# Block-sparse attention and a maxout layer: the first third of three batches' attention rows transposed by TensorE in place of DMA transposes

## The chip, the cores and the metric

The kernel runs on one core of one Trainium2 chip. The metric is device time in microseconds (us) of one execution; of the kernel before there are three timed runs and one profiled execution. Engines are named as in the profile: PE (TensorE, with PEld for its weight loads), DVE (VectorE), ACT (ScalarE), POOL (GpSimd) and SP (SyncE, which here only issues transfers). ACT has a transfer queue as well.

## The reference

Four batches of eight heads attend over 768 positions with head size 64. Each position sees its neighbours closer than 16 and 24 block summaries (the maximum of 32 keys, the mean of 32 values). The result, laid out as 3072 rows of 512, goes through a maxout layer:

```python
k_sum = k.reshape(B, H, nb, 32, D).max(axis=3);  v_sum = v.reshape(B, H, nb, 32, D).mean(axis=3)
scores_l = where(|i - j| < 16, scale * q @ k.T, -1e9)
scores_s = scale * q @ k_sum.T + log(32)
a = softmax(concat([scores_l, scores_s]))
x = (a @ concat([v, v_sum])) laid out as (3072, 512)
out = maximum(x @ w1, x @ w2) @ w_out          # d_model 512, d_ff 1024
```

The kernel uses max(h1, h2) = h1 + relu(h2 - h1): it computes `x @ (w2 - w1)`, takes relu of it (tile `g`), and adds `x @ (w1 @ w_out)` to `g @ w_out`. The product `w1 @ w_out` is made once (tile `w1o`).

## The kernel before, in words

**The work.** For each batch b (0 to 3) and each pair of heads hp (0 to 3), `prep` loads q and k, casts them to bf16 (`cast`), turns them so that the head dimension lies on partitions (`turn`, L463: by PE into a PSUM bank; `dturn`, L467: by a DMA transpose, for six of the sixteen pairs, listed in `CFG["turn"]`), and places keys and block maxima (`place`, `max`, `sums`, `tails`, `wrap`). A batch's 768 positions are cut into three groups (grp 0 to 2) of 256, and each group is done in two halves of four heads. For each half: `scores` (L529), `exp` on ACT (L541), a mask multiplication on DVE (L549, batches 1 to 3), `values` (L569), a reciprocal of the row sums (L587) and their product, the tile x (L590, four blocks of 128 by 128, bf16).

**The step that is changed.** The layer needs x transposed (tile `xt`, one for each batch and group). In batch 0 PE does it: `turn x` is four transposes into a bank (L605), and DVE or ACT copies the bank into `xt` (L258, label `xt`). In batches 1 to 3 SP issues one DMA transpose for each half (L596, label `dxt`, 18 in all).

**The layer.** For each group: `hidden` (L678, four banks of eight products of 256 columns), relu on ACT or DVE (L690, L692), then for each 128 rows `out`: four products `x` with `w1o` and eight with `g` (L715; 512 columns each), a copy out of the bank (L258, `copy out`) and a `store` (L729, L731; on SP's or ACT's queue). The last 128 rows, "320" (batch 3, group 2, half 0), are made in three pieces of 256, 128 and 128 columns. `w1o` is made at L662 from `w1t` and `wo`.

**What sets the order.** Every step is a task in a plan. A table of numbers (`CFG["order"]`) gives the order in which the tasks are issued, a string (`CFG["engines"]`) gives each task's engine, and another (`CFG["slots"]`) which buffer of its ring it writes. Each engine takes its tasks in that order, and waits for what they read and for the buffers that they overwrite. There are 30 `filler` products (L750), which write zeros and are read by nobody; all but two stand on PE ahead of the first 22 us' end.

Of the kernel before, what the change touches and what calls it, by code (L numbers as in the profile page):

```python
# [18 lines left out]


CFG = dict(
    turn="22 23 30 31 32 33", fill=30, apart="",
)
CFG["engines"] = "".join("""
DDPDDDDPPDPDPDPPTTTTTTTTTTTTTTTTTTTTTTTTTTTTTTSSSPAAATDDPSSSADDATADDSSSDDDATAADSSSPPDPTDPDSSDATDSSPATDSSDDTASSDDTDSDSA
SPSDDTATADPPPDPTDTADPADDATDTDDPPPADTATDDPAADTTATTDDTATTATTDDTATTATTDDTDTTATTDDTDTTATTDDTDTTATTDDTASSSASSSDSSSDSSSPADDD
DPTAPDDDAADDDTDTDDPAAAATDTADDPPADTDTDDPAPDDTDTDDAADDTADTTDDSTADTTDDSTADTTDDSTADTTDDSTADTTDDSTADTTDDSSSSASSSASSSASSSADP
DAPAPTADADAPAPDATATDDPDADDTATDDPDPDPSDSDDPDPDSASADDPDTADTTDDSTADTTDDSTADTTDDSTADTTDDSTADTTDDSTADTTDDSSSSDSSSDSSSDSSSDP
ADPAAATAPPDDDPPAPSASDDDPPASASDDAPPPSDSDDADPDSDSADDPDTADTTDDSTADTTDDSTADTTDDSTADTTDDSTADTTDDSTADTTDDSTTATTDTTATTDTTATTA
TTDTTATTTAATTTASTTDTTDTTATTATTTDSTTTDSTTATTDTTATTDTTTAATTTAATATDTATATTTASTTTASTDTATATDTTTASTTTASTATATDTATTTAATTTASTDTA  # L30
TDTATTTAATTTDSTDTATATATTTDSTTTAATATDTATATTTASTTTAATDTATDTATTTASTTTAATDTDTDTDTTTDSTTTDATATATDTATTTAATTTAATTTDSTTTDS
""".split())
CFG["order"] = list(map(int, """
# [28 lines left out]
""".split()))  # L62
CFG["slots"] = "".join("""
62042222021106710531003202313307231146225:92038;61<0042111340176159:02011300112351100237323242320261022522460324040071
0001000221160432210551<47898;6372010411534153241633000262220121202324610426125432206020144162353<002=47:;8>50241030214
34123211222003301214111422034002204241064003223621;<21536:=01>97125053101142010320204231000000501212040203202124342346
2201623730702125441574016062035031561075120162776743420432132341762015540341624532677725412445001541265304420201127162
""".split())
ENG = {"T": "PE", "D": "DVE", "A": "ACT", "P": "POOL", "S": "SP"}

# [25 lines left out]
class Plan:  # L96
# [6 lines left out]
    def op(self, on, fn, read=(), write=(), change=(), touch=(), label=""):  # L103
        t = Task()
        n = t.index = len(self.tasks)
        t.alts, t.letter, t.fn, t.label = on, on[0], fn, label
        if self.engines:
            t.letter = self.engines[n]
            assert t.letter in on, (label, t.letter, on)
        t.new = [*dict.fromkeys((*write, *change))]  # L110
        t.deps = {w for b in (*read, *change) for w in b.writers}
        t.uses = [*dict.fromkeys((*read, *touch, *t.new))]
        for b in t.new:
            b.writers.append(t)
        for b in t.uses:
            b.users.append(t)
            if b.ring and not b.fixed and b not in self.bufs:
                self.bufs.append(b)
        self.tasks.append(t)
        return t  # L120
# [15 lines left out]
def kernel(  # L136
# [31 lines left out]
    def tiles(name, n, shape, dt):  # L168
        return [const.tile(shape, dt, name=f"{name}{i}") for i in range(n)]
# [24 lines left out]
    apart = tiles("apart", 2, [128, H, VW], BF16) if lone else ()  # L194
# [36 lines left out]
    def queue(e):  # L231
        return {"S": nc.sync, "A": nc.scalar, "P": nc.gpsimd}[e]
# [323 lines left out]
    def values(b, hp, grp, pb):  # L556
# [25 lines left out]
        inv, x, half = Buf(invr), Buf(xsr), hp // 2  # L582
        if hp == 0:
# [8 lines left out]
            in0=spread(bank_tile[:, ps.ap, 0:1], [512, 2], [D + 1, 4], [1, D]),  # L592
            in1=spread(inv.ap[:, 0:1, 0:1], [4, 2], [1, 4], [0, D]), op=ALU.mult),
           read=[ps, inv], write=[x], label=f"x {tag}")
        if b > 0:
            op("S", lambda e: queue(e).dma_start_transpose(  # L596
                out=x_t.ap[:, hp:hp + 2, :].rearrange("p h (u n) -> p (h u) n", u=2),
                in_=x.ap[:].rearrange("p h u a d -> p (h u a d)")),
               read=[x], write=[x_t, x_h], label=f"dxt {tag}")
            return  # L600
# [134 lines left out]
    def attention(b):  # L735
        for hp in range(NP):
            prep(b, hp)
        for grp in range(NG):
            for half in range(2):
                on_pe = b == 0  # L740
                ps = Buf(banks, "sc")
                scores(b, 2 * half, grp, ps, on_pe)
                pb = weigh(b, 2 * half, grp, ps, on_pe)
                values(b, 2 * half, grp, pb)
# [67 lines left out]
```

## Time and profile before

| | |
|---|---|
| timed runs | 164.91 us median of 3 (164.22 to 164.93) |
| profiled execution, its own time | 165.06 us |
| its span, first to last instruction | 163.2 us |
| PE busy, share of the span | 152.8 us, 94% |
| DVE, ACT, POOL busy | 111.5, 97.5, 43.9 us |
| granted PE clock | 1.0 |

The profile is read as follows: a row of a group gives the source line, the engine, the operation, what is written and read, the shapes and the count, then the busy time and the mean of one, then idle time of the engine ahead of it. L258 and L256 are the lines of a helper that makes every copy, so those rows are told apart by their tiles. A matmul's shown duration is longer than the step from one matmul to the next, since they are pipelined.

### The profile page before, as it was taken

The page shows a single profiled execution, that of the slowest core. Times are in us where ns is not written, and L with a number is a line of the kernel's source. Part 1 is how long each engine was busy: PE and PEld are TensorE (multiplying, and loading weights), DVE is VectorE, ACT ScalarE, POOL GpSimd, SP SyncE. Part 2 cuts the span into 40 slices and gives each one's busy share as a digit, 9 for nine tenths or more (in the row PEclk, how much of TensorE's full clock was granted, in tenths as well). Part 3 has the DMA queues.
Part 4 walks back from the last instruction along what each step waited for, and adds up shares of the span by engine and source line. Part 5 has one row for each costly group of instructions (what it writes and reads, how often), then busy time and mean ns, then how long its engine had stood idle before and what let it go on. Part 6 is the DMA issues. An engine that isn't in the chain of part 4 may idle for free.

```text
span 163.2 us, 4346 instructions
## 1 busy us (share of the span) xinstructions
PE 152.8 (94%) x1761; PEld 99.9 (61%) x1782; DVE 111.5 (68%) x220; ACT 97.5 (60%) x140; POOL 43.9 (27%) x95
## 2 busy tenths in 40 slices
PE   6977889999999999999999999999999999999990
PEld 2534668888645655588665745868554576686640
DVE  3469999997897899869988576454937967115000
ACT  3369898446529899993999435866659510043121
POOL 6725457003036020069250240000595000000000
PEclk9999999999999999999999999999999999999999
DMA  4999999998999999579899997699996523531752
GB/s 152 324 312 316 263 389 391 395 395 259 281 301 265 308 339 260 89 177 279 114 231 290 320 180 169 120 135 277 229 133 209 128 37 68 161 118 55 233 179 64
DMA packets 67988, 36.48 MB, mean 224 GB/s; under 512 B 54912, under 2 KB 61952, under 8 KB 67968
## 3 DMA queue, kind: packets, MB, share of 16 engines
q1 hardware_dynamic: 66048, 33.43, 77.0%
q10 hardware_dynamic: 1920, 2.77, 5.2%
q8 instruction: 14, 0.23, 0.6%
q14 instruction: 6, 0.05, 0.1%
HBM read 25.18 MB, written 6.29 MB: 193 GB/s over the span
## 4 chain that ended last, share of the span: by engine, by line
PE 55%; issue 15%; DMA 8%; SPq 7%; DVE 6%; POOL 5%; ACT 2%; POOLq 0%; DVEq 0%
PE banks L715 22%; PE banks L678 17%; PE banks L662 4%; SPq L336 4%; DMA land<-in_q_dram 3%; PE banks L569 3%; DMA land<-in_k_dram 3%; POOL vx L256 3%; PE banks L463 3%; PE banks L529 2%; DVE vx L258 2%; POOL kx L258 2%; DVE ks L487 2%; SPq L729 1%; DMA out_dram<-o 1%
## 5 line engine op out<-in xcount | busy, mean ns | idle before, releaser
L678 PE MATMUL banks<-xt,wd 128*128 128x256 bf16 x384 | 45.6, 273 | 0.0
L715 PE MATMUL banks<-wo,g 128*128 128x512 bf16 (+2 forms) x198 | 44.6, 362 | 0.9 <-issue 0.6
L678 PEld LDWEIGHTS <-wd 128*128 128x128 bf16 x384 | 36.9, 98 | 6.9 <-issue 0.3
L715 PEld LDWEIGHTS <-g 128*128 128x128 bf16 x208 | 19.2, 98 | 18.4
L690 ACT ACTIVATE g<-banks 128x512 bf16<-128x512 f32 x28 | 15.7, 596 | 22.2 <-PE banks L678 22.1
L541 ACT ACTIVATE pb<-banks 128x1024 bf16<-128x1024 f32 x24 | 23.7, 1029 | 8.4 <-PE banks L529 8.2
L715 PE MATMUL banks<-w1o,xt 128*128 128x512 bf16 (+2 forms) x96 | 23.6, 362 | 0.6 <-DVE kqb L258 0.2
L692 DVE TENSOR_SCALAR g<-banks 128x512 bf16<-128x512 f32 x20 | 13.5, 685 | 10.4 <-PE banks L678 10.3
L487 DVE TENSOR_REDUCE ks<-kx 128x24 bf16<-128x768 bf16 x16 | 14.9, 947 | 2.7 <-ACT kx L258 2.4
L590 DVE TENSOR_TENSOR xs<-banks,inv 128x512 bf16<-128x512 f32 x24 | 16.4, 689 | 0.5
L258 ACT COPY o<-banks 128x512 f32<-128x512 f32 (+1 forms) x18 | 10.0, 574 | 11.1 <-PE banks L715 7.6
L258 POOL COPY kx<-kx 128x32 bf16<-128x32 bf16 (+1 forms) x16 | 6.5, 422 | 35.9 <-ACT kx L258 20.7
L549 DVE TENSOR_TENSOR pb<-pb,mask 128x1024 bf16<-128x1024 bf16 x18 | 12.2, 693 | 4.3 <-ACT pb L541 4.0
L715 PEld LDWEIGHTS <-xt 128*128 128x128 bf16 x104 | 9.5, 98 | 8.8
L256 POOL COPY vx<-sums 32x396 bf16<-32x396 bf16 x18 | 9.6, 557 | 10.8 <-ACT vx L258 5.5
L750 PE MATMUL banks<-zeros,identity 128*128 128x512 bf16 x29 | 10.3, 465 | 1.6 <-DVE identity L239 1.6
L258 ACT CAST kqb<-land 128x768 bf16<-128x768 f32 x11 | 10.1, 937 | 2.6 <-DMA land<-in_k_dram 2.5
L463 PE MATMUL banks<-ident,kqb 128*128 128x128 f32 x60 | 10.2, 286 | 1.5 <-DVE sums L269 1.1
L258 ACT COPY vx<-vx 32x128 bf16<-32x128 bf16 (+5 forms) x12 | 10.2, 860 | 1.9 <-DVE vx L258 1.7
L463 PEld LDWEIGHTS banks<-ident,kqb 128*128 128x128 f32 x60 | 7.4, 145 | 5.1 <-DVE sums L269 1.5
L258 DVE CAST kqb<-land 128x768 bf16<-128x768 f32 x15 | 8.8, 607 | 2.5 <-DMA land<-in_q_dram 1.3
L258 DVE COPY o<-banks 128x512 f32<-128x512 f32 (+1 forms) x8 | 4.7, 591 | 8.0 <-PE banks L715 6.8
(82 smaller groups left out, 175.7 us busy)
## 6 DMA issues: line engine op xcount, KB each, us to landing
land<-in_k_dram SPq DMA_DIRECT2D x16, 384.0 KB, 5.7
land<-in_v_dram SPq DMA_DIRECT2D x14, 384.0 KB, 5.8
land<-in_q_dram SPq DMA_DIRECT2D x14, 384.0 KB, 5.5
land<-in_moe_w_dram SPq DMA_DIRECT2D x8, 512.0 KB, 8.8
out_dram<-o SPq DMA_DIRECT2D x12, 256.0 KB, 2.6
land<-in_moe_w_out_dram SPq DMA_DIRECT2D x4, 512.0 KB, 11.0
out_dram<-o ACTq DMA_DIRECT2D x7, 256.0 KB, 2.3
w1t<-in_v_dram SPq DMA_DIRECT2D x2, 384.0 KB, 5.3
```

The source lines that it names most:

```text
L256: nc.gpsimd.tensor_copy(out=o[:, n * z:n * z + n], in_=i[:, n * z:n * z + n])
L258: {"D": nc.vector.tensor_copy, "A": nc.scalar.copy, "P": nc.gpsimd.tensor_copy}[e](out=o, in_=i)
L463: nc.tensor.transpose(out=bank(ps)[:, 128 * j:128 * j + 128], in_=src.ap[:].bitcast(F32)[:, 128 * j:128 * j + 128], identity=ident32[:])
L487: op("D", lambda e: nc.vector.tensor_reduce(out=ks.ap[:, 0:nb], in_=free(kt(), 128, [256, NM], [192, 2], [32, 2], [1, 32]), axis=AX.X, op= ...
L541: op("A", lambda e: nc.scalar.activation(out=spread(pb.ap[:, 0, 0:1], [1, 1024]), in_=spread(bank_tile[:, ps.ap, 0:1], [1, 1024]), func=AC ...
L549: on(e).tensor_tensor(out=o.rearrange("p n (u c) -> p n u c", u=2), in0=o.rearrange("p n (u c) -> p n u c", u=2), in1=in1, op=ALU.mult)
L590: op("D", lambda e: nc.vector.tensor_tensor(out=x.ap[:].rearrange("p n u a d -> p n (u a) d"), in0=spread(bank_tile[:, ps.ap, 0:1], [512, ...
L678: nc.tensor.matmul(out=bank(ps)[:, 256 * s:256 * s + 256], lhsT=wd[n // 2][:, c, 256 * (n % 2) + 128 * s:256 * (n % 2) + 128 * s + 128], r ...
L690: nc.scalar.activation(out=o, in_=bank(ps), func=ACT.Relu)
L692: nc.vector.tensor_scalar_max(out=o, in0=bank(ps), scalar1=0.0)
L715: nc.tensor.matmul(out=bank(ps, c1 - c0), lhsT=a, rhs=w, start=(i == j == 0), stop=(i == 2 and j == 3))
L750: nc.tensor.matmul(out=bank(ps), lhsT=identity[:], rhs=zeros[:], start=True, stop=True)
```

## The change

For the groups listed in a new entry, `x="10 20 30"` (group 0 of batches 1, 2 and 3), the early return with the DMA transpose is not taken, so the two halves of each go through `turn x` and the copy `xt`, as in batch 0: six pieces. The task list grows from 822 to 828, and order, engines and slots are new tables. The source lines below the table move by two (L605 is L607 in the changed kernel, L715 is L717).

```diff
 CFG = dict(
-    turn="22 23 30 31 32 33", fill=30, apart="",
+    turn="22 23 30 31 32 33", fill=30, apart="", x="10 20 30",
 )
...
-46 57 8 18 3 48 27 79 10 36 9 58 31 0 1 6 11 13 12 24 2 14 26 68 28 122 15 35 4 59 40 123 132 37 47 126 21 42 127 128
...
+38 97 71 182 163 96 199 73 75 144 164 102 183 67 155 103 72 76 30 200 216 78 184 29 82 161 109 145 185 165 186 151 166
...
-        if b > 0:
+        if b > 0 and f"{b}{grp}" not in CFG["x"].split():
             op("S", lambda e: queue(e).dma_start_transpose(
                 out=x_t.ap[:, hp:hp + 2, :].rearrange("p h (u n) -> p (h u) n", u=2),
                 in_=x.ap[:].rearrange("p h u a d -> p (h u a d)")),
                read=[x], write=[x_t, x_h], label=f"dxt {tag}")
             return
```

The number of tasks on each engine goes from 291 to 297 on PE, 218 to 214 on DVE, 150 to 158 on ACT, 58 to 65 on POOL and 105 to 94 on SP. The first 126 entries of the order are the same in both, and DVE's first 44 tasks (to the end of its first `wd`, 26 us in the profile before).

**First place: batch 1's first group.** In the kernel before, SP's queue holds the group's two DMA transposes (the first two rows) ahead of the transpose of a key tile and those of batch 1's last group (`xt_103`):

```order
L596 DMA_TRANSPOSE xt_102<-xs_97 128x4x128
L596 DMA_TRANSPOSE xt_102<-xs_95 128x4x128
L467 DMA_TRANSPOSE kt_89<-kqb_62 128x6x128
L596 DMA_TRANSPOSE xt_103<-xs_98 128x4x128
L596 DMA_TRANSPOSE xt_103<-xs_96 128x4x128
```

In the changed kernel PE does the first of the two pieces, eight rows, between an `out` product with `g` and an `out` product with `xt`:

```order
L717 MATMUL banks<-wo_138,g_107 128x512
L607 LDWEIGHTS xs_95
L607 MATMUL banks<-identity,xs_95 128x128
L607 LDWEIGHTS xs_95
L607 MATMUL banks<-identity,xs_95 128x128
L607 LDWEIGHTS xs_95
L607 MATMUL banks<-identity,xs_95 128x128
L607 LDWEIGHTS xs_95
L607 MATMUL banks<-identity,xs_95 128x128
L717 LDWEIGHTS xt_101
```

The second piece follows four products later; the same happens in batches 2 and 3, and SP's queue is six DMA transposes shorter.

**Second place: ACT while `w1o` is made (about 42 to 51 us of the profile before).** In the kernel before ACT's queue reads so there; `g` rows are relu, `kx` and `qx` the placing of keys and queries, `w1o` the copy of a finished product:

```order
L690 ACTIVATE g_107<-banks 128x512
L258 COPY kx_69<-banks 128x6x2x64
L258 COPY kx_68<-kx_68 128x32
L258 CAST w1o_141<-banks 128x512
L258 CAST w1o_139<-banks 128x512
L258 COPY qx_74<-banks 128x768
L258 COPY kx_67<-ks_87 128x6x2x32
```

In the changed kernel there stand, between a relu and the placing of the first queries, two casts of `w_out` (`wo`) and the cast of a query tile (`kqb_65`) as well:

```order
L692 ACTIVATE g_107<-banks 128x512 x2
L260 COPY kx_67<-ks_86 128x6x2x32
L260 CAST wo_137<-land_122 128x1024
L260 COPY kx_68<-banks 128x6x2x64
L260 CAST wo_138<-land_123 128x1024
L260 CAST kqb_65<-land_124 128x768
L260 COPY kx_68<-kx_68 128x6x2x32
L260 COPY qx_74<-banks 128x768
```

Of these, the casts of `wo_137` and `wo_138` were POOL's and DVE's, and that of the query tile DVE's. PE's `w1o` products read `wo_137` and `wo_138`, and its next `turn` reads `kqb_65`.

**Third place: the end.** In the kernel before ACT's queue ends with the copy of a whole 128 by 512 result and its two stores (rows that wrap round the sequence go apart):

```order
L258 COPY o_109<-banks 128x256
L729 DMA out_dram<-o_109 128x256
L258 COPY o_108<-banks 128x512
L258 COPY o_110<-banks 128x512
L729 DMA out_dram<-o_110 112x512
L731 DMA out_dram<-o_110 16x512
```

In the changed kernel the last result on PE is a piece of 128 columns of the rows "320", and ACT's queue ends so:

```order
L692 ACTIVATE g_105<-banks 128x512
L260 COPY o_108<-banks 128x512
L731 DMA out_dram<-o_108 128x512
L260 COPY o_109<-banks 128x512
L260 COPY o_111<-banks 128x512
L731 DMA out_dram<-o_111 128x512
L260 COPY o_113<-banks 128x128
L731 DMA out_dram<-o_113 128x128
```

The result whose rows need two stores is done earlier, and the last copy and store are a quarter as wide. The relu in the first row stands behind three copies and five stores of ACT since the relu before it.

**A filler.** One of the two late fillers (ahead of a `turn k` in the middle of batch 0's `hidden` work) stands in the changed kernel between `turn q03` and `values 0011`, about 19 us into the profile before.

More of the change, by code (lines that the diff above doesn't have):

```diff
@@ L21 @@
 CFG = dict(
-    turn="22 23 30 31 32 33", fill=30, apart="",
+    turn="22 23 30 31 32 33", fill=30, apart="", x="10 20 30",
 )
 CFG["engines"] = "".join("""
[L25 to L31, printed above, removed]
+DDPDDDDPPDPDPDPPTTTTTTTTTTTTTTTTTTTTTTTTTTTTTTSSSPAAATDDPSSSADDATADDSSSDDDATAADSSSPPDPTDPDSSDATASSPATDSSDATASSDATDSDSA
+SASADTATADPPPDPTDTADPADDATDTDDPPPADTATDDPAADTTATTDDTATTATTDDTDTTATTDDTDTTATTDDTDTTATTDDTDTTATTDDTDSSSPSSSASSSDSSSDDDDP
+DPTADAADDDADDTATADDDPDPTATDDPPAAPTDTADDPDDDTATADDADATADTTDDTATADTTDDTATADTTDDSTADTTDDSTADTTDDSTADTTDDSSSSASSSASSSDSSSD
+DPPADDDTDPAAPPPDPDTATADPAPDATPTDDAAAAASPSDDADAASPSADADATADTTDDTATADTTDDTDTADTTDDSTADTTDDSTADTTDDSTADTTDDSSSSPSSSPSSSAS
+SSPPPPPPPATDPADPPPPPPSASDDAPAPSASDDDAADSASDDDPDPSASADDPATADTTDDTDTADTTDDTDTADTTDDSTADTTDDSTADTTDDSTADTTDDSTTDTTDTTATTA
+TTATTDTTATTDTTTASTTTDATTDTTATTATTDTTTAATTTAATTDTTATTDTTATTTDATTTAATATDTATDTTTDSTTTDATATATATATTTASTTTDSTDTDTDTDTTTASTTT
+DATATATATDTTTDSTTTASTDTATDTDTTTDSTTTAATATDTDTDTTTDATTTASTDTDTDTATTTDATTTAATATATDTDTTTAATTTASTATATDTDTTTAATTTAATTTAATTT
+DA
 """.split())
@@ L36 @@
 156 56 198 60 146 81 180 147 34 148 90 129 64 124 45 149 157 158 63 125 65 62 159 61 39 154 131 17 55 20 181 91 160 66
[25 rows of a table removed]
[25 rows of a table added]
 """.split()))
 CFG["slots"] = "".join("""
[L64 to L67, printed above, removed]
+62042222021102610531003202313307231146225:92038;61<0062112340176158:01011300112351100237323242320261022722421024040071
+00021102211604340355769293:4;5<42012601011331040131301211122562213736022062300256222321001404010<03084=56129;402724012
+042412331033110222041401416061056302300440242420243611>0112<7;5:=38111435002013303524123102214201235406006614124010030
+3020364421413652002705541363530170612424471016011312361023200553251061227216152173332250433713572106345010166437151715
+430554
 """.split())
```

49 rows, old and new, of the table turn are left out of this document.

## The prediction

> **What bounds the kernel now.** I read the page first, for the engines' shares and the clock, then busy time by stretch, then PE's waits, and last the end of the chain. The page:
>
> ```profile
> span 163.2 us, 4346 instructions
> ...
> PE 152.8 (94%) x1761; PEld 99.9 (61%) x1782; DVE 111.5 (68%) x220; ACT 97.5 (60%) x140; POOL 43.9 (27%) x95
> ...
> PE   6977889999999999999999999999999999999990
> ...
> PEclk9999999999999999999999999999999999999999
> DMA  4999999998999999579899997699996523531752
> ```
>
> PE is busy nearly everywhere, at the full clock. DMA is as full for the first 65 us and loosens after that, so two resources could be the bound. Busy time by stretch (columns: PE, PEld, DVE, ACT, POOL, with instruction counts, then clock and DMA share) and PE's own waits tell them apart:
>
> ```profile
> 0.00:21.00 21.00, 16.66 (x159) 9.38 (x161) 14.22 (x35) 13.55 (x20) 11.55 (x39) 1.00 0.96 275
> 21.00:40.00 19.00, 18.79 (x277) 15.57 (x278) 18.33 (x37) 11.99 (x17) 6.05 (x11) 1.00 1.02 370
> 40.00:53.00 13.00, 12.89 (x74) 7.06 (x73) 10.50 (x17) 7.62 (x14) 4.35 (x8) 1.00 1.03 283
> 53.00:72.00 19.00, 18.58 (x320) 11.31 (x323) 16.64 (x35) 18.42 (x24) 2.56 (x5) 1.00 0.94 245
> 72.00:125.00 53.00, 52.16 (x607) 34.68 (x615) 36.90 (x70) 36.58 (x53) 19.37 (x36) 1.00 0.94 208
> 125.00:159.00 34.00, 33.63 (x343) 21.88 (x340) 14.94 (x29) 8.72 (x14) 0.00 (x0) 1.00 0.41 119
> ...
> PE banks L750 <- DVE identity L239: 1.6, 1, 1.6
> PE banks L463 <- DVE sums L269: 1.1, 1, 1.1
> PE banks L529 <- DVE qx L258: 0.9, 1, 0.9
> PE banks L715 <- issue: 0.8, 5, 0.2
> PE banks L569 <- DVE qx L258: 0.4, 1, 0.4
> ```
>
> PE idles 4.3 us in the first 21 us (21.00 less 16.66); those are the waits for DVE in the lower rows, the first two products and the first scores and values. After 21 us it misses 1 to 2% of each stretch, and most of that isn't idleness: the page has 1761 matmul records beside 1782 weight loads, so 21 are missing, and the 0.8 us put down to "issue" is five holes of 0.2 us, a 512-column product each. No row has PE waiting for a transfer. So from 21 us to the end PE works without a stop, and the time is PE's work plus the start ahead of it plus the tail behind it.
>
> **PE's work.** It gains six pieces of four transposes and loses a filler from its full part:
>
> ```profile
> 28.94 0.22 PE banks L605 x4
> ...
> 36.34 0.22 PE banks L750
> ...
> L605 PE MATMUL banks<-identity,xs 128*128 128x128 bf16 x24 | 2.3, 219 | 0.0
> ```
>
> In the chain of waits, which shows steps and not durations, one piece of batch 0 takes 0.22 us. Six of them take 6 x 0.22 = 1.32 us, and nothing covers them: there is no idle PE left to put them in. The filler costs 0.22 us where it stands (36.34 us). In the changed kernel it stands ahead of a product of values at 19 us, and behind that PE waits 0.4 us for DVE (the last row of PE's waits), so there it costs nothing; without that cover it would cost its 0.22 us again. The start is otherwise the same, since order and engines don't differ up to there and DVE's tasks are the same to 26 us. Sum for PE: 1.32 - 0.22 = +1.10 us. Excursions from full-height products to scores and values and back I count as equal, 20 in each order.
>
> A rule speaks against this price. The Trainium skill, "TensorE: Matmul & The Clock Gate", Part 4: PE-mode transpose, gives about 275 ns for one 128 by 128 bf16 transpose inside a kernel. By that the 24 would take an estimated 6.6 us. The trace has four in 0.22 us in the place where they were, so the measured step decides; what speaks for the rule is taken up below.
>
> **What the transfers give back.** These rows are the removed transposes, how long they took to land, and the two copies that replace them, by DVE or by ACT:
>
> ```profile
> L596 SPq DMA_TRANSPOSE xt<-xs x18: 1189/1224/2547, 64.6 to 137.8; - x18
> ...
> DMA to landing us min/median/max: 2.4/2.6/4.7
> ...
> L258 ACT COPY xt<-banks 128x512 bf16<-128x512 bf16 x3 | 1.7, 582 | 2.0 <-PE banks L605 2.0
> ...
> L258 DVE COPY xt<-banks 128x512 bf16<-128x512 bf16 x3 | 1.2, 416 | 0.0
> ```
>
> SP's queue loses 6 x 1.22 = 7.3 us, and what it holds behind them (loads and key turns of batches 2 and 3, stores) can go out earlier. Since PE waited for none of it, that is worth 0 us; the same holds for x coming sooner (0.22 + 0.58 us in place of 2.6). The six copies cost 6 x 0.42 to 6 x 0.58 = 2.5 to 3.5 us of DVE or ACT, which from 72 us on idle 16 of 53 us and then 19 to 25 of 34: nothing, as long as PE has other products in hand. For batch 1 it has 24 small products and four steps of values between the second piece and the first `hidden`.
>
> **The tail.** Here are the last product, its copy and its two stores, then the rows from which the new ones are priced:
>
> ```profile
> 157.16 1.89 PE L715 MATMUL banks<-wo,g 128*128 128x512 bf16 x8
> 159.08 0.58 ACT L258 COPY o<-banks 128x512 f32<-128x512 f32 x1 [2.00 <-DMA out_dram<-o]
> 159.70 0.34 ACTq L729 DMA_DIRECT2D out_dram<-o  x1
> 160.08 0.44 ACTq L731 DMA_DIRECT2D out_dram<-o  x1
> ...
> L258 ACT CAST sums<-banks 128x128 bf16<-128x128 f32 x5 | 1.3, 263 | 0.3 <-PE banks L424 0.3
> ...
> out_dram<-o SPq DMA_DIRECT2D x2, 64.0 KB, 2.7
> ...
> out_dram<-o ACTq DMA_DIRECT2D x3, 32.0 KB, 3.2
> ```
>
> PE ends at 157.16 + 1.89 = 159.05, so the tail is 163.2 - 159.05 = 4.15 us, and 163.2 - 160.08 = 3.12 us of it come after the last issue begins. In the changed kernel the last twelve products are 128 by 128, three times the four-product step, 3 x 0.22 = 0.66 us. Counted from PE's end: ACT starts the copy of the whole result before them at -0.62 and ends it at -0.04, issues its store until +0.30, copies the last 128 columns (263 ns, the nearest ACT row of that size) until +0.60, and begins the last issue at +0.64. With the same 3.12 us behind it the tail is 3.76 us, 0.4 less; if the last store lands sooner by what a 64 KB store has over a 32 KB one (3.2 - 2.7), it is 3.26, 0.9 less. I take -0.6 us, nearer to the first, since the store of the whole result lands beside it.
>
> **The sum.** The profiled execution's own time is 165.06 us, 1.86 over its span. 165.06 + 1.10 - 0.6 = 165.56; it stood 0.15 above the median 164.91, which makes 165.4 us for a median, or +0.3%. That is no change as far as a measurement of this kernel can tell, which is about 0.5%, or 0.82 us either way: 164.1 to 165.7. With the tail's bounds it is 165.1 to 165.6. PE's steps may also fit together a little better or worse in the new order: between 21 and 159 us it is shown busy for 136.05 of 138 us, and a tenth of the missing 1.95 either way makes 164.9 to 165.8. A small part of that lies over 165.7.
>
> **The rivals.**
>
> *ACT late around w1o (slower).* Rows for the second place:
>
> ```profile
> L258 ACT CAST kqb<-land 128x768 bf16<-128x768 f32 x11 | 10.1, 937 | 2.6 <-DMA land<-in_k_dram 2.5
> ...
> L258 ACT COPY kx<-banks 128x768 bf16<-128x768 bf16 x3 | 2.4, 798 | 5.6 <-PE banks L463 5.6
> ...
> L258 ACT COPY kx<-ks 128x384 bf16<-128x384 bf16 x3 | 1.6, 517 | 0.0
> ...
> L258 ACT CAST wo<-land 128x1024 bf16<-128x1024 f32 x1 | 1.0, 1048 | 0.0
> ...
> 44.82 3.67 PE banks L662 x17
> ```
>
> From the first `sums` copy to the query cast ACT has 0.52 + 1.05 + 0.80 + 1.05 + 0.94 = 4.35 us of work. PE has, from the turn whose bank the third of these empties to the turn that reads the cast, five tasks of four 512-column products, each 4 x 3.67 / 17 = 0.86: 4.3 us. If ACT begins no later than PE, the two end together and PE loses nothing; each tenth that ACT begins later is a tenth of idle PE, and one more cast ahead of it (0.94) makes 0.9 us. That ACT idled 5.4 of 13 us here (40 to 53) speaks against it, that these casts come on top of that speaks for it. Price 0.8 us: 166.2, slower than before. It decides from about 0.3 us of lateness.
>
> *ACT late at the end (slower).* The relu of the third place waits in ACT's queue behind three copies (0.58, 0.58 and 0.37) and five issues (four of 0.34, one of 0.44); with the two relus (0.60 each) that makes 4.5 us. PE has six tasks of 0.86, 5.2 us, before the product that reads it. Slack 0.6 us; but an issue can take longer:
>
> ```profile
> 153.14 1.35 ACTq L729 DMA_DIRECT2D out_dram<-o  x1
> ...
> L690 ACT ACTIVATE g<-banks 128x512 bf16<-128x512 f32 x28 | 15.7, 596 | 22.2 <-PE banks L678 22.1
> ...
> L258 ACT COPY o<-banks 128x256 f32<-128x256 f32 x1 | 0.4, 372 | 2.9 <-PE banks L715 2.9
> ```
>
> One such issue adds 1.0, so PE waits 0.4 to 0.5 us: 165.9.
>
> *The transposes do not overlap.* If each held PE for its whole recorded duration, the 219 ns of the L605 row, 24 of them would take 5.3 in place of 1.3 us: 165.4 + 4.0 = 169.4. This is the mechanism of the rule above. Against it stand the 0.22 us for four and that the row has no idle time ahead of it.
>
> *Transfers mattered after all (faster).* Then a wait of PE that the profile hides must go. Taking all 4.3 us of early idleness as open to change, a quarter of it, 1.1 us, would bring 164.3, and a third 164.0. Against it: these waits are for DVE, and the work there is the same in both. The Trainium skill, "VectorE: DVE Perf Modes", Rules for kernel authors, would have a 128 by 128 transpose on TensorE where PSUM will do as its destination. That holds for the path of x (2.6 against 0.8 us) and not for an engine that is full.
>
> **How the numbers follow.** The forecast has 0.68, of which 0.10 lies over 165.7. ACT late around `w1o` has 0.18, ACT late at the end 0.06, transposes that do not overlap 0.02, and faster 0.06. Slower is 0.10 + 0.18 + 0.06 + 0.02 = 0.36, the same 0.58, faster 0.06. The range 164.7 to 166.4 holds the forecast's 164.9 to 165.8 and both ACT cases; it leaves out 169.4 and the faster case, and the ends of each.
>
> **What would show it.** In the profile after: pieces of L607 that step 0.22 us and sit without idle time in PE's chain; PE without waits after 21 us and 1.1 us later at its end (160.15), or a little less; the tail 3.3 to 3.8 us. A wait of PE for ACT at 42 to 54 us, at L463 or L662, would show the first rival, and one at the last L717 products the second. PE waiting for `xt` would say that six copies are not free. The prediction is wrong if PE ends before 159.5, since then I don't know what its work is, or if the time leaves 164.1 to 166.4.

## The result, and the profile after

The changed kernel took 165.70 us (median of 20 runs, 164.47 to 168.06), the kernel before, beside it on the same chip, 164.59 us (20 runs, 163.59 to 167.38). The ratio is 1.0076 (95% interval 1.0053 to 1.0098), that is +1.25 us (0.87 to 1.61). So the change made the kernel slower, by little more than a measurement can tell; the forecast had +0.3% and "no change". The time itself, 165.7 us, lies 0.3 us from the forecast and inside its range. Disturbed runs are left out of the ratios here and below.

The profiled execution took 164.92 us with a span of 163.1 us, 0.78 us below its own median, and the one of before stood 0.47 above the median of these 20 runs. So the two spans, 163.1 and 163.2, hide the difference, and the comparison has to go by parts. The page of the changed kernel:

```profile
span 163.1 us, 4434 instructions
...
PE 156.2 (96%) x1806; PEld 101.5 (62%) x1806; DVE 109.3 (67%) x216; ACT 97.8 (60%) x143; POOL 58.2 (36%) x121
...
PE   5997999999999999999999999999999999999991
...
PEclk9999999999999999999999999999999999999999
DMA  4999999999999997458979996778971255410434
```

All 1806 matmul records are there this time. Of the 45 more than before, 24 are the new transposes, and 21 are records that the profile before lacks, so 156.2 us against 152.8 isn't PE's growth. DMA stays at nine tenths for the first 61 us and loosens after, much as before. Busy time by stretch (columns as in the prediction):

```profile
21.00:40.00 19.00, 18.92 (x266) 15.65 (x265) 16.47 (x33) 13.85 (x19) 5.87 (x10) 1.00 1.05 380
40.00:53.00 13.00, 13.00 (x73) 6.96 (x72) 9.36 (x18) 10.69 (x16) 5.68 (x11) 1.00 1.16 328
53.00:72.00 19.00, 18.83 (x329) 11.51 (x328) 15.38 (x34) 16.79 (x24) 2.10 (x5) 1.00 0.77 211
72.00:125.00 53.00, 52.98 (x657) 35.08 (x655) 40.26 (x72) 35.66 (x55) 33.01 (x58) 1.00 0.88 191
125.00:159.00 34.00, 34.00 (x301) 21.83 (x300) 12.68 (x26) 5.78 (x11) 0.00 (x0) 1.00 0.33 100
```

From 40 to 53 us, where ACT took over three casts and the first rival saw PE waiting, PE is busy for 13.00 of 13 us. What is missing otherwise lies, but for 0.02 us, in two stretches, 0.08 us at 21 to 40 and 0.17 us at 53 to 72. PE's waits in the whole span:

```profile
PE banks L752 <- DVE identity L241: 1.6, 1, 1.6
PE banks L531 <- DVE qx L260: 0.8, 1, 0.8
PE banks L571 <- DVE qx L260: 0.4, 1, 0.4
PE banks L465 <- ACT kqb L260: 0.3, 1, 0.3
PE banks L571 <- DVE xs L592: 0.2, 1, 0.2
```

The first four belong to the start, as before. The last is new: a step of values that waits for DVE's product `xs`. The chain of waits (start, length, work) shows this place and a second one, and the new pieces of L607:

```profile
27.01 0.38 PE banks L571 x16
27.39 0.34 PE banks L607 x4
27.73 0.17 issue
27.91 0.22 DVE inv L589
28.12 0.02 issue
28.15 0.70 DVE xs L592
28.85 0.04 issue
28.89 0.60 PE banks L680 x4
...
64.83 0.70 DVE xs L592
65.53 0.04 issue
65.58 0.45 PE banks L571 x16
66.02 1.83 PE banks L717 x8
67.86 0.22 PE banks L607 x4
68.08 0.86 PE banks L717 x4
68.94 0.22 PE banks L607 x4
```

Twice the chain leaves PE for DVE. PE writes a step of values into a bank, DVE turns it into `xs` (a reciprocal and a product), and PE wants that same bank again (the slots in the kernel's tables say which): at 28.85 us for four products of `hidden`, at 65.53 for the next step of values. In the kernel before the chain stays on PE from 26 to 31 and, but for two steps of 0.05 us, from 62 to 69 us. By the start times on PE, each against the usual step between such tasks, the first wait costs 0.24 us and the second 0.33. The first lies ahead of all six pieces, so it comes of the new order and not of them. The duration of a matmul hides most of both, as it lasts longer than its step, so the waits view has only 0.2 and nothing. The new pieces (67.86 us and later) step 0.22 us each, with PE's work on both sides; in batch 2 the two stand side by side. The tail, in the timeline (start, duration, engine, line, what):

```profile
159.06 0.61 PE L717 MATMUL banks<-wo,g 128*128 128x128 bf16 x8
159.65 0.34 ACTq L731 DMA_DIRECT2D out_dram<-o  x1
160.03 0.27 ACT L260 COPY o<-banks 128x128 f32<-128x128 f32 x1 [0.41 <-PE banks L717]
160.33 0.34 ACTq L731 DMA_DIRECT2D out_dram<-o  x1
```

PE ends at 159.06 + 0.61 = 159.67, so the tail is 163.1 - 159.67 = 3.43 us in place of 4.15. The last issue begins 0.66 us after PE's end, and the span ends 2.77 us after that (3.12 before).

### The profile page after: what moved, and what is told of

The parts are those of the page before. It is cut to its first block, busy times and chain, and to the rows that moved or that the text cites. A ratio compares the mean times of both kernels' runs of the same rounds, so it can differ in the third digit from the quotient of the medians.

```text
span 163.1 us, 4434 instructions
## 1 busy us (share of the span) xinstructions
PE 156.2 (96%) x1806; PEld 101.5 (62%) x1806; DVE 109.3 (67%) x216; ACT 97.8 (60%) x143; POOL 58.2 (36%) x121
## 4 chain that ended last, share of the span: by engine, by line
PE 81%; DVE 8%; DMA 3%; SPq 3%; ACT 2%; issue 1%; ACTq 0%; DVEq 0%
PE banks L717 36%; PE banks L680 26%; PE banks L664 4%; PE banks L571 4%; PE banks L531 4%; DMA land<-in_k_dram 3%; DVE vx L260 3%; PE banks L465 3%; SPq L338 2%; PE banks L607 2%; DVE pb L551 2%; DVE xs L592 1%; PE banks L641 1%; DVE ks L489 1%; PE banks L520 1%; PE banks L426 1%
## 5 line engine op out<-in xcount | busy, mean ns | idle before, releaser
L717 PE MATMUL banks<-wo,g 128*128 128x512 bf16 (+2 forms) x208 | 46.6, 363 | 0.0
L692 ACT ACTIVATE g<-banks 128x512 bf16<-128x512 f32 x22 | 12.8, 601 | 32.2 <-PE banks L680 30.7
L717 PEld LDWEIGHTS <-g 128*128 128x128 bf16 x208 | 19.2, 98 | 18.3
L717 PE MATMUL banks<-w1o,xt 128*128 128x512 bf16 (+2 forms) x104 | 24.5, 363 | 0.0
L694 DVE TENSOR_SCALAR g<-banks 128x512 bf16<-128x512 f32 x26 | 17.4, 687 | 8.3 <-PE banks L680 8.2
L258 POOL COPY vx<-sums 32x396 bf16<-32x396 bf16 x26 | 14.8, 594 | 5.1 <-DVE sums L260 4.6
L717 PEld LDWEIGHTS <-xt 128*128 128x128 bf16 x104 | 9.5, 98 | 8.2
L260 DVE COPY o<-banks 128x512 f32<-128x512 f32 (+1 forms) x11 | 7.0, 638 | 10.5 <-PE banks L717 10.5
L260 ACT CAST kqb<-land 128x768 bf16<-128x768 f32 x14 | 13.0, 938 | 0.3 <-DMA land<-in_k_dram 0.2
L258 POOL COPY vx<-vx 64x792 bf16<-64x792 bf16 (+2 forms) x16 | 12.2, 789 | 1.9 <-DVE vx L260 1.6
L260 ACT COPY o<-banks 128x512 f32<-128x512 f32 (+2 forms) x15 | 8.2, 556 | 6.7 <-PE banks L717 5.8
L258 POOL CAST kqb<-land 128x256 bf16<-128x256 f32 (+1 forms) x18 | 8.1, 481 | 7.5 <-ACT g L692 5.1
L258 POOL CAST vx<-land 128x384 bf16<-128x384 f32 x12 | 6.6, 573 | 10.7 <-issue 5.8
L571 PEld LDWEIGHTS <-pb 128*64 128x64 bf16 x384 | 7.4, 110 | 4.5 <-issue 2.1
```

The lines of the kernel that those rows point to most:

```text
L258: nc.gpsimd.tensor_copy(out=o[:, n * z:n * z + n], in_=i[:, n * z:n * z + n])
L260: {"D": nc.vector.tensor_copy, "A": nc.scalar.copy, "P": nc.gpsimd.tensor_copy}[e](out=o, in_=i)
L571: nc.tensor.matmul(out=av(n)[64 * par:64 * par + 64, u, a, :], lhsT=pb.ap[r, at, 64 * par:64 * par + 64], rhs=rhs, start=start, stop=stop)
L692: nc.scalar.activation(out=o, in_=bank(ps), func=ACT.Relu)
L694: nc.vector.tensor_scalar_max(out=o, in0=bank(ps), scalar1=0.0)
L717: nc.tensor.matmul(out=bank(ps, c1 - c0), lhsT=a, rhs=w, start=(i == j == 0), stop=(i == 2 and j == 3))
```

## The experiments

Tasks are named in the diffs as in the plan: `turn x120` is the transpose piece of batch 1, pair 2, group 0; `outg1 021` the second half of the `g` products of batch 0, group 2, half 1.

**Two kernels, several executions.** The span depends on the execution as much as on the change. The last `sums` product of batch 0 marks the end of the start; with it a span divides into the start, the stretch from there to PE's end, and the tail. Both kernels were profiled again, unchanged.

> The changed kernel once more, for a second profile beside these. Both theories: ratio 1.0076 within 0.003. Theory B: where the first scores and values come late (about 21.5 us), fewer waits of PE after 25 us than the 0.7 us of the first profile (0.2 to 0.3); where they come early (20.2), more (over 1.5). Theory A: the same 0.7 us.

> The kernel before, for another profile. Its median span is 162.4 to 162.8 us, while the first profile had 163.2. Theory S (executions differ in the start alone): the step from the first sums of batch 0's last pair to PE's end stays 137.4 to 137.5 us, and the start is about 20.9. Theory B (an earlier start is partly given back in waits): with a start before 21 us that stretch is 137.7 to 138.1.

> As e8_before_a, a further execution: theory S 137.4 to 137.5 us in the stretch, theory B more with an early start.

> The changed kernel, for another profile; its median span is 163.7 us, and both profiles so far have 163.1 with a start of 20.7 to 20.9. Theory S: the stretch stays 138.8 to 138.9 us and the span follows the start. Theory B: where the start is earlier than 20.7 the stretch is longer than 139, where it is 21.5 it is 138.3 to 138.5.

> As e9_changed_a, a further execution: theory S 138.8 to 138.9 us in the stretch, theory B more with an early start and less with a late one.

The mark, in the earliest execution of the kernel before and the latest of the changed one (its second row here):

```profile
20.26 0.51 PE L387 MATMUL banks<-vx,amean 128*128 128x128 bf16 x6
```

```profile
19.66 0.50 PE L389 MATMUL banks<-vx,amean 128*128 128x128 bf16 x6
23.42 0.52 PE L389 MATMUL banks<-vx,amean 128*128 128x128 bf16 x6
```

| kernel (its own time, us) | start | PE's end | stretch | tail |
|---|---|---|---|---|
| before (165.06) | 21.59 | 159.05 | 137.46 | 4.15 |
| before, again (163.41) | 20.26 | 157.41 | 137.15 | 4.1 |
| before, again (163.83) | 20.47 | 157.94 | 137.47 | 4.2 |
| changed (164.92) | 20.88 | 159.67 | 138.79 | 3.43 |
| changed, again (164.90) | 20.74 | 159.67 | 138.93 | 3.43 |
| changed, again (167.51) | 23.42 | 162.27 | 138.85 | 3.4 |
| changed, again (165.32) | 20.92 | 160.06 | 139.14 | 3.4 |

The start varies by 3.2 us, the stretch within one kernel by 0.35. The means of the stretch are 137.36 and 138.93, so the change adds 1.57 us there and takes 0.7 from the tail: +0.87 us at an equal start. In rounds, the changed kernel took 165.45 us again, at a ratio of 1.0065 (1.0034 to 1.0096), or +1.07 us. That agrees with 0.87; the first ratio's 1.25 has 0.87 at the edge of its interval. Of the 1.57, 24 transposes less a filler are 1.11 (24 x 0.0555 = 1.33, less 0.22) and the two waits 0.57, which all four profiles of the changed kernel have; that makes 1.68, 0.1 more than measured.

The starts of PE's products, each against the usual step, show where the 0.1 is. The waits in the stretch add up to 0.19 us in the mean before (0.26, 0.00 and 0.30 us) and to 0.78 in the changed kernel (0.66, 0.77, 0.72 and 0.96). Without them the stretches are 137.15 to 137.19 us and 138.13 to 138.19. So PE's work grew by 0.98 us and its waits by 0.59.

The late start of 23.42 has a wait of its own, of PE for a cast of keys:

```profile
PE banks L465 <- DVE kqb L260: 1.6, 1, 1.6
```

DVE, which makes that cast, waits for the loads: first the late execution's row from the waits of the first 21 us, then that of the one with the start of 20.26:

```profile
DVE kqb L260 <- DMA land<-in_k_dram: 3.1, 2, 2.3
```

```profile
DVE kqb L258 <- DMA land<-in_k_dram: 1.5, 2, 0.9
```

The key loads hold DVE 1.6 us longer, which is half of the 3.2. The other half comes behind the loads, where in this execution alone the granted clock falls. Its row of the clock, in 40 slices of the span, and a step of its chain of waits:

```profile
PEclk9987999999999999999999999999999999999998
...
12.11 1.71 PE banks L752 x4
```

Its mean from 10 to 15 us is 0.66, where every other profile has 1.00, and four fillers take 1.71 us, where one takes 0.22 at the full clock. Why the clock fell is not shown. The order is the same in both kernels up to there, so the loads and the clock are no effect of the change, and without this execution the starts lie between 20.26 and 21.59.

**The pieces alone.** The order of before, with the six DMA transposes made by PE, put ahead of products that PE can do meanwhile, and their copies by DVE or ACT:

```diff
-    turn="22 23 30 31 32 33", fill=30, apart="",
+    turn="22 23 30 31 32 33", fill=30, apart="", x="10 20 30",
 PE's order, by tasks:
+turn x120, turn x100
 outg1 021
...
+turn x220, turn x200
 outg0 121
...
+turn x300, turn x320
 outg1 311
```

> The change alone: order, engines and slots of the kernel before, and only the six DMA transposes replaced by PE pieces and copies, put in where banks and copying engines were free (batch 1 at about 69 us, batch 2 at 95.6, batch 3 at 139 of the profile before). Theory (PE's work adds up: six pieces of 0.22 us, no filler moved, the old tail): PE ends 1.3 us later, time +1.3 us, ratio 1.008. Rival (the new order costs, the transposes do not): ratio 1.000 to 1.003. Rival (the transfers taken off the queues give something back): under 1.004.

It took 165.82 us, 1.0079 of before (1.0048 to 1.0110), or +1.30 us (0.79 to 1.81). The pieces' step is 1.33. Its busy time by stretch:

```profile
53.00:72.00 19.00, 19.00 (x328) 11.51 (x328) 17.00 (x37) 18.42 (x24) 2.55 (x5) 1.00 0.78 209
72.00:125.00 53.00, 53.00 (x600) 34.82 (x596) 37.27 (x70) 36.50 (x54) 18.34 (x35) 1.00 0.91 190
```

PE has no idle time in these 72 us, and its stretch is 138.84 us, 1.48 above the mean of before. By the starts of PE's products 0.28 us of that are waits at 125 us, against 0.19 in the mean of before, so nearly all of the pieces' price is PE's own work. The order needs no fault for the change to lose.

**The transfers alone.** The kernel before without the six DMA transposes; POOL fills those tiles with zeros:

```diff
+        if b > 0 and grp == 0:
+            op("P", lambda e: nc.gpsimd.memset(x_t.ap[:, hp:hp + 2, :], 0.0), write=[x_t, x_h], label=f"dxt {tag}")
+            return
```

> The kernel before without its six DMA transposes of group 0 of batches 1 to 3: POOL, idle there, writes zeros into those tiles instead (x of these groups is left out). No PE piece takes their place. Theory (PE waited for none of them): ratio 1.000, within 0.002. Rival (relief of the queues is worth something): ratio under 0.997.

It took 165.24 us, 1.0032 of before (1.0000 to 1.0065): no relief from six transfers less. Its busy time where they had been:

```profile
53.00:72.00 19.00, 19.00 (x325) 11.49 (x325) 16.76 (x35) 18.43 (x23) 3.54 (x7) 1.00 0.86 232
72.00:125.00 53.00, 53.00 (x618) 34.62 (x616) 36.58 (x70) 36.59 (x54) 19.71 (x40) 1.00 0.92 202
```

At nearly the same start as in the profile of before (21.53 and 21.59) DMA's share falls from 0.94 to 0.86 in the first of them, and PE, which was full, stays full; the stretch is 137.18 us. Why the runs are a little slower, if they are, its profile doesn't show.

**A quarter of the transposes.** The changed kernel with one transpose in each of the six pieces in place of four, and a copy that repeats that block:

```diff
-            for n in range(4):
+            for n in range(4 if b == 0 else 1):
```

> The changed kernel with its order, but each of the six pieces makes one of its four transposes, and the copy repeats that block four times (so three quarters of x of group 0 of batches 1 to 3 are left out). Theory (PE's work adds up): 18 transposes of 0.056 us fewer, -1.0 us against the changed kernel, ratio to before 1.0015 if the changed kernel stands at 1.0076. Rival (the new order costs): unchanged at 1.007 to 1.008, with waits of PE in its place.

It took 165.03 us, 1.0036 of before (1.0005 to 1.0067), between the two expectations. PE does 18 x 0.0555 = 1.00 us less, and the profile shows what took its place:

```profile
PE banks L531 <- DMA kt<-kqb: 0.8, 1, 0.8
PE banks L531 <- DVE xs L592: 0.8, 1, 0.8
```

At 93 us scores of batch 2 wait for DVE's `xs` (the second row), and DVE had itself just waited 0.6 us for a DMA transpose of keys; at 121 us scores of batch 3 wait for such a transpose (the first row). By the starts of PE's products the two places lose 0.9 us each, and 0 to 0.2 us together in the four profiles of the changed kernel. The two waits for `xs` at 28 and 65 us are there as well, so they belong to the order and not to the number of transposes. This execution also began early, at 20.20 us against 20.88, so at 93 us PE is ahead by more than the transposes left out, and its stretch, 139.65 us, is even longer than the changed kernel's. The runs, 0.3 to 0.4% below the two ratios of the changed kernel, got back 0.5 to 0.7 us of the 1.00. So here the price of the pieces came back only in part; one profile doesn't show how much of the loss is due to its early start.

**The tail alone.** The order of before with another end: the rows "321" and "300", whole, ahead of the last 128 columns of "320", and the store of "300" issued by ACT in place of SP:

```diff
 PE's order, by tasks, after outg1 301:
-outx 300, outg0 300, outx 320 256, outg0 320 256, outg0 320 128, outg1 320 128,
-outg1 320 256, outg1 300, outx 321, outg0 321, outg1 321
+outx 320 256, outg0 320 256, outx 321, outg1 320 256, outg0 321, outg1 321,
+outx 300, outg0 300, outg1 300, outg0 320 128, outg1 320 128
```

> The kernel before with DMA transposes, and only its last 24 steps in another order: the rows 321 go out earlier, and PE's last products are those of a piece of 128 columns, copied by DVE and stored by SP, while the store of the rows 300 goes to ACT's queue. Theory (the tail is worth what the two profiles show, 4.15 against 3.4 to 3.5 us): PE ends at the same time, tail 3.3 to 3.6, time -0.6 to -0.9 us, ratio 0.995 to 0.996. Rival (stores side by side land no sooner): ratio 1.000.

It took 164.08 us, 0.9981 of before (0.9951 to 1.0011). The end of its timeline:

```profile
157.64 0.59 ACT L260 COPY o<-banks 128x512 f32<-128x512 f32 x1 [1.98 <-DMA out_dram<-o]
158.09 0.29 DVE L260 COPY o<-banks 128x128 f32<-128x128 f32 x1 [7.45 <-PE banks L717]
158.25 0.36 ACTq L731 DMA_DIRECT2D out_dram<-o  x1
158.41 0.35 SPq L731 DMA_DIRECT2D out_dram<-o  x1
```

PE ends at 158.05 of 161.5 us: a tail of 3.45, 0.7 less than before, as in the changed kernel and without its other parts. In this execution a wait of 0.45 us at 89 us, for DVE's masking of `pb`, gives nearly two thirds of that back. The runs' -0.31 us has both expectations in or at the edge of its interval (-0.81 to +0.18), so the tail's gain is shown by the profiles and not by these runs.

**The parts together, in the old order.** The pieces as above, this tail, and the late filler moved from `hidden` to ahead of `turn q02`, where PE waits anyway:

```diff
 PE's order, by tasks:
+filler
 turn q02
...
-filler
 turn k12
```

> The order of the kernel before with three edits: the six PE pieces in place of the DMA transposes, the tail in the other order, and the late filler moved to 19 us. Theory B (of the changed kernel's +1.25 us only +0.4 is PE's work and tail, the rest is its new order, in which PE arrives at steps that are not ready): 1.33 - 0.22 - 0.7 = +0.4 us, ratio 1.0025, some 0.8 us faster than the changed kernel. Theory A (work and tail are all there is, and the changed kernel should have come out at +0.4): the same as the changed kernel within 0.3 us, so both between 1.003 and 1.006.

It took 165.21 us, 1.0044 of before (1.0017 to 1.0072), or +0.72 us; its stretch is 138.56 us. The sum of the parts, 1.33 - 0.22 - 0.7 = +0.41, is inside the interval. It has neither of the two waits for `xs`, and the two ratios of the changed kernel lie 0.2 to 0.3% above it, 0.3 to 0.5 us, about the two waits' 0.57. The intervals overlap; the waits are shown by the profiles, their effect on the runs is not by these alone. No run has the new order with the DMA transposes kept.

**A version without the pieces.** The same without the six pieces, that is the order of before with the new tail and the moved filler; twice, the second time the same kernel again:

> As the last, without the six PE pieces: the kernel before with the tail in the other order and the late filler moved. If work and tail add up: -0.22 - 0.7 = -0.9 us, ratio 0.9945. If an earlier PE only waits at steps that are not ready: 0.997 to 1.000, with waits in its profile.

> The kernel of e6 once more, to narrow its interval: the kernel before with the tail in the other order and the late filler moved, DMA transposes kept. The tail has been 0.7 us shorter in every profile that has it. If work, waits and tail add up, -0.7 to -0.9 us, ratio 0.9945 to 0.996; the first five rounds gave 0.9979 (0.9948 to 1.0009). If the tail's gain is lost elsewhere in most executions: 0.998 to 1.000.

It took 163.91 and 164.10 us, 0.9979 (0.9948 to 1.0009) and 0.9977 (0.9944 to 1.0010): the lowest ratios here, but neither interval leaves out 1, and both stay short of the 0.9945 that tail and filler add up to (0.7 + 0.22 = 0.92 us), which only the second interval reaches. In the second profile PE waits at 124 us (the first row) and at 90 us (the second):

```profile
PE banks L531 <- POOL kx L260: 0.3, 1, 0.3
PE banks L571 <- DVE pb L551: 0.3, 1, 0.3
```

Its chain of waits leads from the masking of `pb` at 90 us back to a load of values:

```profile
82.75 5.63 DMA land<-in_v_dram
...
88.40 0.56 DVE vx L260
88.96 1.21 DVE pb L551 x2
```

Its stretch is 138.42 us, with a start of 20.45. By the starts of PE's products the place at 90 us loses 0.6 us and that at 124 us, where the chain comes from POOL's copies, 0.7. The first profile has a start of 20.98, a stretch of 137.54 and neither of these waits (one of 0.45 us at 30 us instead). So an execution that is early can be held by a load or by POOL, and the same kernel's stretch can differ by 0.9 us. It need not be: the earliest execution of the kernel before (20.26) has no wait behind its start. How often that happens, and whether it is why the runs show only 0.34 and 0.38 of the 0.92 us, stays open.

## Why the time was right and the difference was not

The time lay in the stated range, and PE ended at 159.67 us, not before the 159.5 that was named as a sign of being wrong. What failed is the difference from before: +0.3% and no change, where +0.76% was measured, clear of zero.

**PE's work, +1.10 us: right.** The pieces step 0.22 us in the chain, and alone, in the old order, they cost 1.30 us (0.79 to 1.81) against 1.32. In the changed kernel PE's work grew by 0.98 us, so its steps fit together about 0.1 better there. PE's end came 0.6 us later than before, not 1.1, because that execution's start was 0.7 us earlier (20.88 against 21.59).

**The transfers' relief, 0: right.** Six transfers less brought nothing (1.0032, 1.0000 to 1.0065), and the changed kernel's stretch is longer, not shorter, than before.

**"PE without waits after 21 us": this step failed.** The sum took new waits of PE as 0 in the likeliest case, and gave the fit of PE's steps 0.2 us either way. Measured are two waits, 0.24 and 0.33 us, in all four profiles of the changed kernel, and with smaller ones 0.59 us more than in the kernel before. I had compared the two orders for ACT's queue and for SP's, and not for how soon PE comes back to a bank that DVE still reads. The mechanism was PE returning too soon to a bank that DVE still reads; the two rivals about the new order both named ACT.

**The tail, -0.6 us: right, a little small.** It measured -0.7 in the profiles, inside the bounds -0.4 and -0.9. The last issue began 0.66 us after PE's end, as worked out (0.64), and the span's end followed 2.77 us after it, between the 3.12 and the 2.62 of the two bounds.

**The base: too high, and it hid the failed step.** I took the profiled execution as 0.15 us above the median of three runs; it stood 0.47 above the median of 20. By the true base the sum would have been 165.06 + 0.50 - 0.47 = 165.1, and with the waits and the measured tail 165.1 + 0.57 - 0.1 = 165.6, where 165.70 was measured. So the time came out within 0.3 us by luck, by two errors of opposite sign, and the difference from before, +0.49 against 1.25, did not. The parts as forecast, with the two waits, add up to 1.10 + 0.57 - 0.7 = +0.97, and the stretches less the tail to +0.87; the rest of 1.25 is inside the interval and has no row that shows it.

**The rivals.** ACT late around `w1o`: no wait of PE from 40 to 53 us, so ACT came in time there. ACT late at the end: none at the last L717 products. Transfers that mattered after all: contradicted by the experiment without them. Transposes that do not overlap would have cost 5.3 us alone where 1.30 were measured. The Trainium skill, "TensorE: Matmul & The Clock Gate", Part 4: PE-mode transpose, gives about 275 ns for one inside a kernel. Here the row shows 219 ns for one, but four take 0.22 us of PE's time, at a granted clock of 1.00, so the measurement decides against multiplying that duration by the count. The Trainium skill, "VectorE: DVE Perf Modes", Rules for kernel authors, would have such transposes on TensorE where PSUM will do as the destination: here that is the loss, since PE is the engine that is full.

## What to carry to other kernels

Work that moves from a queue nobody waits for to the engine that is full can cost its whole step, however short it is: here 24 x 0.056 us. In a new order, look for how soon the full engine returns to a buffer that another engine still reads, on every engine that empties such buffers, and not only for the queues that got more work. Where a change is worth less than 1%, split the profiles at a mark behind the varying start before comparing them, and take the base from many runs.

## What the runs showed of the hardware

The start of the same instructions varied from 20.26 to 21.59 us between executions, and was 23.42 in one in which DVE waited 3.1 us for early key loads and the granted clock was 0.66 from 10 to 15 us. The 138 us behind the start repeated within 0.35 us in the two kernels here, and within 0.9 us in the version without the pieces. A 128 by 128 transpose on PE steps 0.056 us in a row of four, though its row shows 219 ns. A profile can lack 21 of its matmul records in one execution and none in the next, of the same kernel: the holes read as five to seven waits for "issue" of 0.2 us each, and they aren't idle time.
